# Third product of the first steps removed, small GpSimd copies moved behind the gate, and the transform of even k split once more

## The chip, the cores and the metric

The kernel runs on one NeuronCore of one Trainium2 chip. The time is device microseconds of one launch. Below, TensorE is PE (its weight loads PEld), VectorE is DVE, ScalarE is ACT, GpSimd is POOL and SyncE is SP in the profile's rows. A step's instructions wait for each other across engines by semaphores; each engine runs its own queue in program order.

## What is computed

```python
def _attn_ref(x):                      # x: 8 x 3136 x 256, float32
    X = np.fft.fft(x, axis=1)
    X = np.fft.fft(X, axis=2)
    return X.real.astype(np.float32)

def _moe_ref(x, w_in, conv_w, w_out):  # 256 -> 1024 -> 256, 3 taps
    h = np.maximum(x @ w_in, 0.0)
    hp = np.concatenate([zeros, h, zeros], axis=1)
    for k in range(3):
        conv_out += conv_w[k][None, None, :] * hp[:, k:k + S, :]
    gate = 1.0 / (1.0 + np.exp(-conv_out))
    return (h * gate @ w_out).astype(np.float32)
```

`reference` feeds the first function's output to the second. All arithmetic of the kernel is float32.

## The kernel before

**The transform.** The input is real and only the real part of the two-dimensional transform is used, so per batch two arrays are enough, for k from 0 to 1568: a cosine sum P and a sine sum Q over the sequence. The row k of h needs P and Q added, the row 3136 - k needs them subtracted. The sum over the sequence is shortened by folding: VectorE adds and subtracts the quarters of the sequence and the mirrored features (`fold_ops`, 14 pieces a batch, lines 154 to 193) until 98 (or 99) rows of the array `w` in 4 groups q are left for even k and for odd k. In the piece `feats`, GpSimd copies the one feature that has no mirror (L187, 98x4 or 99x4 elements) and clears another (L189).

A batch's transform is eight units (`units`), each of a few matrix products of a table with `w` into one PSUM bank, then a copy by ScalarE where two halves have to be combined, then two VectorE additions that write P (`pt`) or Q (`qt`). For odd k the sum over n is split into even n and odd n: `odd_even` does the n that are even, on a quarter of the k, and mirrors them (two contiguous additions, L309 and L311); `odd` does the odd n (L321 and L323, which write every second column). For even k, `even(sn, c)` takes the two classes of even k one after the other, c = 0 and c = 1, each with four products of 197 or 196 columns, one copy (L286) and two additions that write every fourth column (L290 and L293).

**The steps.** Each batch has 4 chunks of columns k and, for each chunk, 8 blocks of 128 hidden features: 32 steps a batch, 256 in all. A step s has these parts, spread over four cycles of the loop:

- `seed` (L653, ACT) writes the contribution of feature 128 to the bank `pa`.
- `products` (PE): `pb` = G1 times Q (L667), then `pa` += G0 times P.
- `copies` (ACT): `nb` gets `pb` for the front rows k and minus `pb` for the mirrored back rows, two copies (L685).
- `combine` (DVE): two custom instructions (L696), each the sum of `pa` and `nb` clipped at zero, write the front and the back of the tile `h`; `row_of` allocates `h` and clears its edges in a batch's first chunk (L663, POOL).
- `first_tap` (L702, ACT), then `tap` twice (L707, DVE, two SBUF inputs): the convolution, in the tile `g`.
- `sigmoid` (L720, ACT), in two parts.
- `gate`: g times h, the first half by VectorE (L728), the other by GpSimd (L727), with a rest by GpSimd in a batch's last chunk (L730).
- `mm2` (PE): six or more products of 256 columns with `w_out`, added up over the 8 blocks in the banks `po`, which ScalarE copies out (L747) and SP stores.

In batch 0 the steps 3 to 19 are done in another way (`triple`): PE adds `pb`'s product a third time, into `pa`, so that `pa` holds the front rows complete; ACT writes the front of `h` with a Relu (L682) and copies only minus twice `pb` for the back (L680); VectorE's L696 runs once, for the back.

**The order.** The engines' order is written out by hand. Cycle t of the loop issues `sigmoid` of step t - 2, "first" work, `products` and `copies` of step t + 1, "act" work, `combine` of step t, `seed` of t + 2, `first_tap` of t, `tap` 1 of t - 1, "dve" work, `tap` 2 of t - 1, `gate` of t - 2, "load" work, `mm2` of t - 3 and "pe" work. The named places take side work from the table `side`: the folds of batch b are spread over the cycles before `ends[b]` at "dve" (with GpSimd's L187 and L189 inside them), the units of batch b over the cycles after it (matmuls at "pe", copies at "act", additions at "dve"), and the loads of the next batch, four indirect gathers on GpSimd's queue among them (L132), at "load". Batch 1's folds lie in cycles 9 to 19 and its units in cycles 20 to 29. Cycles 0 to 9 also widen weights (L524 to L542). Batch 0's folds and units come ahead of the loop.

Of the kernel before, what the change touches and what calls it, by code (L numbers as in the profile page):

```python
# [9 lines left out]
F32 = mybir.dt.float32  # L10
# [16 lines left out]

TRIPLE = 3, 20  # L30
RC = 56
NQ = 8
CUTS = (0, 384, 768, 1152)
# [4 lines left out]
def kernel(  # L38
# [103 lines left out]
    def fold_ops(b):  # L142

        def half(h):
            k = slice(0, NP if h == 0 else KR)
            qs = slice(2 * h, 2 * h + 2)

            def t():
                return xh[b, h]

            def pair(m):
                def f():
                    a, r = t()[k, m:m + 2], t()[k, 7 - m:5 - m:-1, ::-1, :]
                    vt(a[:, :, :, 1:D], a[:, :, :, 1:D], r[:, :, :, D - 1:0:-1], op=ALU.add)  # L157
                    if m == 2:
                        a, r = t()[k, 0:4], t()[k, 7:3:-1, ::-1, :]
                        vt(a[:, :, :, 0], a[:, :, :, 0], r[:, :, :, 0], op=ALU.add)  # L160
                return f

            def flat(i, j):
                return t()[k, i:j].rearrange("p s q d -> p (s q d)")

            def both(to, op):
                def f():
                    vt(flat(to, to + 2), flat(0, 2), flat(2, 4), op=op)  # L168
                return f

            def evens():
                vt(flat(0, 1), flat(4, 5), flat(5, 6), op=ALU.add)
                vt(flat(1, 2), flat(4, 5), flat(5, 6), op=ALU.subtract)

            def feats(odd):
                def f():
                    if h == 0 and odd:
                        wt[b] = [wp.tile([P, 4, HQ, P], F32, name="w", tag="w%d" % i) for i in range(2)]
                        if b == 0:
                            ea[b] = ep.tile([P, 2, HQ], F32, name="ea", tag="ea")  # L180
# [5 lines left out]
                    vt(w[k, 2:4, qs, 0:P - 1], lo, hi, op=ALU.subtract)  # L186
# [9 lines left out]
            return [pair(0), pair(2), both(6, ALU.subtract), feats(1), both(4, ALU.add), evens,  # L196
                    feats(0)]

        return half(0) + half(1)

# [63 lines left out]
    def product(o, w, st, q, cols, start, stop):  # L264

        def f(p):
            k = KR if q == HQ - 1 else NP
            mm(p[o], w(k, q), table(k, st, q, cols), start, stop)
        return f

    def units(b):
        def w(i):
            return lambda k, q: wt[b][i // 4][0:k, i % 4, q, :]

        a_ = {}
# [91 lines left out]
        def store():  # L367
            nc.sync.dma_start(out=ed[b:b + 1, 0:NK], in_=er[b])

        return (begin, [odd_even(1), odd(1), even(1, 0), even(1, 1), feature(), odd_even(0), odd(0),  # L370
                        even(0, 0), even(0, 1)], row, flip, store)

    class Feature:

# [280 lines left out]
    def triple(s):  # L655

        return s[0] == 0 and TRIPLE[0] <= s[1] * NF + s[2] < TRIPLE[1]

    def row_of(s):
        hs[s] = hp.tile([P, HW], F32, name="h", tag="h")  # L660
        w = chunks[s[1]].w
# [3 lines left out]
    def products(s):  # L665
        b, c, f = s
        ch, n, fs = cut(s)  # L667
        pb[s] = psb.tile([P, 512], F32, name="pb", tag="pb")
        mm(pb[s][:, 0:n], G[0:P - 1, 1, fs], PQ[b][1][0:P - 1, ch.k0:ch.k1], True, True)
        mm(pa[s][:, 0:n], G[:, 0, fs], PQ[b][0][:, ch.k0:ch.k1], False, not triple(s))  # L670
        if triple(s):
            mm(pa[s][:, 0:n], G[0:P - 1, 1, fs], PQ[b][1][0:P - 1, ch.k0:ch.k1], False, True)

    def copies(s):

        ch, n, fs = cut(s)
        p = pb.pop(s)
        nb[s] = nbp.tile([P, 2, HN], F32, name="nb", tag="nb")
        if triple(s):
            act(nb[s][:, 1, ch.cols], p[:, ch.cols], AF.Copy, scale=-2.0)  # L680
            row_of(s)
            act(hs[s][:, ch.front], pa[s][:, ch.fcols], AF.Relu)  # L682
        else:
            for i, cols in enumerate((ch.fcols, ch.cols)):
                act(nb[s][:, i, cols], p[:, cols], AF.Copy, scale=-1.0 if i else 1.0)  # L685

    def combine(s):

        ch, n, fs = cut(s)
        a, c = pa.pop(s), nb.pop(s)  # L690
        if not triple(s):
            row_of(s)
        h = hs[s]
        for i, (to, cols) in enumerate(((h[:, ch.front], ch.fcols), (h[:, ch.back][:, ::-1], ch.cols))):
            if i or not triple(s):
                nc.vector._custom_dve(TENSOR_ADD_SAT, out=to, in0=a[:, cols], in1=c[:, i, cols],  # L696
                                      s0=BIG, s1=0.0)

    def first_tap(s):
        n = chunks[s[1]].w - 2  # L700
# [63 lines left out]
    begin()  # L764

    nc.gpsimd.memset(PQ[0][1][96:P, :], 0.0)
    for f in fold_ops(0):
        f()

    odds = [us[j] for j in (0, 1, 5, 6)]  # L770
# [99 lines left out]
        at(cs[-1] - 2, "load", lambda b=b: spread(b, range(len(chunks) - 1)))  # L870
        at(per * b + 1, "load", lambda b=b: spread(b, [len(chunks) - 1]))
    for b in range(1, B):
        ops = fold_ops(b)
        c0, n = ends[b - 1], ends[b] - ends[b - 1]
        cs = [free(c0 + j * n // len(ops)) if b > 1 else c0 + j * n // len(ops) for j in range(len(ops))]
        assert cs[-1] < ends[b] and (b > 1 or cs[7] > NF + 3)
# [16 lines left out]
    for t in range(n + LAG):  # L893
# [94 lines left out]
```

## Time and profile before

| | us |
|---|---|
| median of 5 runs (lowest, highest) | 1198.54 (1197.32, 1199.39) |
| the profiled execution | 1199.47 |
| its span, first to last instruction | 1197.7 |

| group | count | mean ns |
|---|---|---|
| PE L93, `po` from `wout`, 256 columns | 3072 | 379 |
| PE L93, `pb` and `pa`, 387 columns and others | 512 each | 496, 494 |
| DVE L707, the taps | 512 | 1130 |
| DVE L696, the custom sum | 495 | 558 |
| DVE L728 / POOL L727, the gate's halves | 256 / 256 | 572 / 1012 |
| ACT L685, copies of `pb` | 478 | 499 |
| ACT L682, Relu of the front, 386 and 385 columns | 17 | 493, 492 |
| POOL L187, copies of one feature | 32 | 1088 |
| POOL L189, clears | 28 | 98 |
| ACT L286, copies for even k | 32 | 322 to 331 |

A float32 product is two instructions on TensorE, and a group's mean time counts each from its start to its modelled end, so that neighbours overlap; the distance from start to start is shorter than the mean. The same holds for VectorE and ScalarE: the last 0.1 us or so of an instruction lies under the next one, and the chain of waits shows the distance. The granted TensorE clock was 1.00 in all but the last of the 30 us stretches, where work ends.

### The profile page before, as it was taken

How to read it: one execution, taken by the hardware profiler on the slowest of the kernel's cores; microseconds unless marked ns; L12 is line 12 of the kernel's file. 1: busy time of each engine (PE TensorE's matmuls, PEld its weight loads, DVE VectorE, ACT ScalarE, POOL GpSimd, SP SyncE). 2: the span in 40 equal slices, each digit the busy share in tenths (PEclk: the TensorE clock that was granted, in tenths of full speed). 3: DMA queues.
4: the chain of work that ended last, by engine and by line, in shares of the span. 5: the costliest groups of instructions: out<-in, count | busy, mean ns of one | idle time of the engine just before them, and what ended most of it. 6: DMA issues, size and time to landing. Idle time of an engine off the chain costs nothing.

```text
span 1197.7 us, 15377 instructions
## 1 busy us (share of the span) xinstructions
PE 1170.3 (98%) x4836; PEld 901.8 (75%) x4836; DVE 1128.6 (94%) x1625; ACT 884.0 (74%) x1840; POOL 476.8 (40%) x540
## 2 busy tenths in 40 slices
PE   4999999999999999999999999999999999999998
PEld 2776777777777777777777777777777777777776
DVE  7899999999999999999999999999998988899996
ACT  2677667777777777777777777777776777788884
POOL 5225556464263433624245243632234222342224
PEclk9999999999999999999999999999999999999999
DMA  9812323112031211202021010310000100110000
GB/s 220 197 35 81 82 29 107 57 54 81 1 99 41 69 39 43 79 14 81 27 88 52 27 54 27 99 36 27 27 31 24 32 27 27 47 34 27 27 27 31
DMA packets 70067, 66.07 MB, mean 55 GB/s; under 512 B 28107, under 2 KB 57683, under 8 KB 69987
## 3 DMA queue, kind: packets, MB, share of 16 engines
q1 hardware_dynamic: 64349, 51.98, 15.3%
q0 software_dynamic: 5120, 12.85, 3.5%
q8 instruction: 38, 0.62, 0.2%
q10 hardware_dynamic: 518, 0.28, 0.1%
q14 instruction: 42, 0.34, 0.1%
HBM read 39.33 MB, written 25.74 MB: 54 GB/s over the span
## 4 chain that ended last, share of the span: by engine, by line
PE 84%; DVE 11%; issue 2%; ACT 1%; POOL 1%; DMA 0%; ACTq 0%; DVEq 0%; SPq 0%; POOLq 0%
PE po L93 51%; PE pb L93 13%; PE pa L93 12%; PE pd L93 8%; DVE g L707 5%; DVE h L696 1%; DVE g L728 1%; POOL xh L132 1%; DVE xh L157 0%; ACT nb L685 0%; DVE xh L168 0%; DVE w L186 0%; DVE raw L539 0%; DVE wout L532 0%; ACT os L747 0%
## 5 line engine op out<-in xcount | busy, mean ns | idle before, releaser
L93 PE MATMUL po<-wout,g 128*128 128x256 f32 x3072 | 705.9, 379 | 5.0 <-DVE g L728 5.0
L93 PEld LDWEIGHTS po<-wout,g 128*128 128x128 f32 x3072 | 580.9, 190 | 149.3 <-issue 17.9
L707 DVE SCALAR_TENSOR_TENSOR g<-h,cw,g 128x770 f32<-128x770 f32 (+1 forms) x512 | 578.7, 1130 | 6.2 <-ACT g L702 2.4
L727 POOL TENSOR_TENSOR g<-g,h 128x385 f32<-128x385 f32 (+1 forms) x256 | 258.8, 1012 | 633.6 <-ACT g L720 439.2
L685 ACT ACTIVATE nb<-pb 128x386 f32<-128x386 f32 (+2 forms) x478 | 212.8, 499 | 162.9 <-PE pb L93 162.4
L720 ACT ACTIVATE g<-g 128x385 f32<-128x385 f32 (+2 forms) x512 | 244.6, 530 | 99.8 <-DVE g L707 96.1
L696 DVE CUSTOM_DVE_ANT_0 h<-pa,nb 128x386 f32<-128x386 f32 (+2 forms) x495 | 256.6, 558 | 3.1 <-POOL h L663 3.1
L702 ACT ACTIVATE g<-h,cw 128x770 f32<-128x770 f32 (+1 forms) x256 | 244.1, 954 | 0.0
L93 PE MATMUL pb<-qt,G 127*128 127x387 f32 (+2 forms) x512 | 212.7, 496 | 1.6 <-ACT G L622 1.6
L93 PE MATMUL pa<-pt,G 128*128 128x387 f32 (+2 forms) x512 | 211.8, 494 | 0.0
L653 ACT ACTIVATE pa<-eb,ge 128x387 f32<-128x387 f32 (+2 forms) x256 | 154.6, 604 | 0.8 <-ACT ft L458 0.6
L93 PEld LDWEIGHTS pa<-pt,G 128*128 128x128 f32 x512 | 96.8, 189 | 73.6 <-issue 18.4
L728 DVE TENSOR_TENSOR g<-g,h 128x385 f32<-128x385 f32 (+1 forms) x256 | 146.3, 572 | 3.0 <-ACT g L720 3.0
L93 PE MATMUL pd<-tab,w 98*128 98x196 f32 (+3 forms) x448 | 126.7, 374 | 0.0
L132 POOL DMA_INDIRECT xh<-in_x_dram,idx x64 | 106.3, 1662 | 13.3 <-issue 9.8
L93 PEld LDWEIGHTS pb<-qt,G 127*128 127x128 f32 x512 | 93.9, 190 | 19.6 <-ACT G L622 2.4
L93 PEld LDWEIGHTS pd<-tab,w 98*128 98x128 f32 (+1 forms) x448 | 84.7, 191 | 12.3
L730 POOL TENSOR_TENSOR left<-g,h 128x64 f32<-128x64 f32 x64 | 65.5, 1024 | 0.0
L747 ACT COPY os<-po 128x256 f32<-128x256 f32 x196 | 57.7, 392 | 9.3 <-PE po L93 4.7
L187 POOL COPY w<-xh 98x4 f32<-98x4 f32 (+1 forms) x32 | 34.8, 1088 | 39.1 <-DVE xh L168 28.4
L157 DVE TENSOR_TENSOR xh<-xh 98x1020 f32<-98x1020 f32 (+1 forms) x32 | 39.5, 1240 | 2.5 <-DMA xh<-in_x_dram,idx 2.5
L168 DVE TENSOR_TENSOR xh<-xh 98x1024 f32<-98x1024 f32 (+1 forms) x32 | 39.0, 1218 | 0.1
(118 smaller groups left out, 367.9 us busy)
## 6 DMA issues: line engine op xcount, KB each, us to landing
out_dram<-os SPq DMA_DIRECT2D x192, 128.0 KB
xh<-in_x_dram SPq DMA_DIRECT2D x16, 784.0 KB
eb<-ed SPq DMA_DIRECT2D x16, 193.5 KB
tab<-dft_seq_dram SPq DMA_DIRECT2D x4, 589.5 KB
raw<-in_moe_w_in_dram SPq DMA_DIRECT2D x4, 512.0 KB
raw<-in_moe_w_out_dram SPq DMA_DIRECT2D x1, 2048.0 KB
eb<-ed SPq DMA_DIRECT2D x8, 209.0 KB
eb<-ed SPq DMA_DIRECT2D x7, 193.0 KB
```

What stands on the lines that cost most here:

```text
L93: nc.tensor.matmul(o, l, r, start=start, stop=stop, skip_group_check=True)
L132: nc.gpsimd.indirect_dma_start(out=xh[b, h][0:NP, 7 - m].rearrange("p q d -> p (q d)"), out_offset=None, in_=bass.AP(tensor=x.tensor, offs ...
L653: act(pa[s][:, 0:n], eb[b, c], AF.Copy, scale=ge[:, f:f + 1])
L685: act(nb[s][:, i, cols], p[:, cols], AF.Copy, scale=-1.0 if i else 1.0)
L696: nc.vector._custom_dve(TENSOR_ADD_SAT, out=to, in0=a[:, cols], in1=c[:, i, cols], s0=BIG, s1=0.0)
L702: act(gs[s], hs[s][:, 0:n], AF.Copy, scale=cw[:, 0, s[2]:s[2] + 1])
L707: stt(out=g, in0=h[:, k:k + n], scalar=cw[:, k, f:f + 1], in1=g, op0=ALU.mult, op1=ALU.add)
L720: act(gs[s][:, c], gs[s][:, c], AF.Sigmoid)
L727: gt(g[:, p], g[:, p], h[:, p], op=ALU.mult)
L728: vt(g[:, v], g[:, v], h[:, v], op=ALU.mult)
L730: gt(left[:, f, b % 2 * LEFT:(b % 2 + 1) * LEFT], g[:, r], h[:, r], op=ALU.mult)
L747: nc.scalar.copy(out=osb[:, j % 2], in_=pt[:, j % 2])
```

## The change

- `triple` is gone. Steps 3 to 19 are done as all others: two products, two copies by ScalarE, two L696 on VectorE, `row_of` in `combine`.
- `feats` no longer holds GpSimd's copy and clear for batches 1 to 7. `single(odd)` does them; the loop runs it in the same cycle at a new place, "pool", which stands behind `gate` and ahead of "load". Batch 0 keeps them in `feats`.
- `even(sn, 0)` and `even(sn, 1)` become `even_even(sn)` and `even(sn)`. `even_even` takes the even n (groups q = 3 and 1) for both classes of even k on half of the columns: four products of 99 or 98 columns that write every second column of the bank, one copy by ScalarE, and two contiguous additions that make the sum and its mirror. `even` takes the odd n (q = 2 and 0): two times two products of 197 or 196 columns, again into every second column, no copy, and two additions of 393 and 392 columns that write every second column of P or Q. The number of units, of products and of additions stays; their place in the schedule too.

```diff
-TRIPLE = 3, 20
...
+            def single(odd):
+
+                def f():
+                    w, s = wt[b][odd], 6 * odd
+                    nc.gpsimd.tensor_copy(w[k, 0:2, qs, 0], t()[k, s:s + 2, :, 0])
+                    if b:
+                        nc.gpsimd.memset(w[k, 2:4, qs, P - 1:P], 0.0)
+                return f
...
-                    nc.gpsimd.tensor_copy(w[k, 0:2, qs, 0], v[:, :, :, 0])
                     if b:
-                        nc.gpsimd.memset(wt[b][odd][k, 2:4, qs, P - 1:P], 0.0)
-                    elif odd:
+                        return
+                    single(odd)()
+                    if odd:
...
+            ops = [pair(0), pair(2), both(6, ALU.subtract), feats(1), both(4, ALU.add), evens, feats(0)]
+            return ops, {3: single(1), 6: single(0)}
...
-        def even(sn, c):
-            n = HO // 2 + 1 - c
-            nh = HO // 2
-            cols = slice(c, HE, 2)
-            mms = [product((slice(0, P), slice(j * n, (j + 1) * n)), w(2 * sn + c), sn, q, cols, q == qs[0], q == qs[1])
-                   for j, qs in enumerate(((3, 1), (2, 0))) for q in qs]
+        def even_even(sn):
+
+            n = HO // 2 + 1
+            mms = [product((slice(0, P), slice(j * n + c, (j + 1) * n, 2)), w(2 * sn + c), sn, q, slice(c, n, 2),
+                           True, True) for j, q in ((0, 3), (1, 1)) for c in range(2)]
 
             def copy(p):
-                a_[sn, c] = asp.tile([P, HO + 2], F32, name="as", tag="as")
-                nc.scalar.copy(out=a_[sn, c][:, 0:n], in_=p[:, 0:n])
+                a_["v", sn], a_["e4"] = [asp.tile([P, HO + 2], F32, name="as", tag="as") for _ in range(2)]
+                nc.scalar.copy(out=a_["e4"][:, 0:n], in_=p[:, 0:n])
 
             def fin(p):
-                a, bb, t = a_[sn, c], p[:, n:2 * n], PQ[b][sn]
-                vt(t[:, 2 * c:Q4 + 1:4], a[:, 0:n], bb, op=ALU.add)
-                hi = t[:, M - 2 * c:Q4:-4]
-                x0, x1 = (bb[:, 0:nh], a[:, 0:nh]) if sn else (a[:, 0:nh], bb[:, 0:nh])
-                vt(hi, x0, x1, op=ALU.subtract)
+                a, e4, e2 = a_["v", sn], a_["e4"], p[:, n:2 * n]
+                vt(a[:, 0:n], e4[:, 0:n], e2, op=ALU.add)
+                x0, x1 = (e2[:, 0:n - 1], e4[:, 0:n - 1])[::1 if sn else -1]
+                vt(a[:, HO:n - 1:-1], x0, x1, op=ALU.subtract)
             return Unit(b, mms, copy, fin)
 
+        def even(sn):
+
+            mms = [product((slice(0, P), slice(c, HE, 2)), w(2 * sn + c), sn, q, slice(c, HE, 2), q == 2, q == 0)
+                   for c in range(2) for q in (2, 0)]
+
+            def fin(p):
+                a, bb, t = a_["v", sn][:, 0:HE], p[:, 0:HE], PQ[b][sn]
+                vt(t[:, 0:Q4 + 1:2], a, bb, op=ALU.add)
+                x0, x1 = (bb, a) if sn else (a, bb)
+                vt(t[:, M:Q4:-2], x0[:, 0:HO], x1[:, 0:HO], op=ALU.subtract)
+            return Unit(b, mms, lambda p: None, fin)
...
-        mm(pa[s][:, 0:n], G[:, 0, fs], PQ[b][0][:, ch.k0:ch.k1], False, not triple(s))
-        if triple(s):
-            mm(pa[s][:, 0:n], G[0:P - 1, 1, fs], PQ[b][1][0:P - 1, ch.k0:ch.k1], False, True)
+        mm(pa[s][:, 0:n], G[:, 0, fs], PQ[b][0][:, ch.k0:ch.k1], False, True)
...
-        if triple(s):
-            act(nb[s][:, 1, ch.cols], p[:, ch.cols], AF.Copy, scale=-2.0)
-            row_of(s)
-            act(hs[s][:, ch.front], pa[s][:, ch.fcols], AF.Relu)
-        else:
-            for i, cols in enumerate((ch.fcols, ch.cols)):
-                act(nb[s][:, i, cols], p[:, cols], AF.Copy, scale=-1.0 if i else 1.0)
+        for i, cols in enumerate((ch.fcols, ch.cols)):
+            act(nb[s][:, i, cols], p[:, cols], AF.Copy, scale=-1.0 if i else 1.0)
...
-            if i or not triple(s):
-                nc.vector._custom_dve(TENSOR_ADD_SAT, out=to, in0=a[:, cols], in1=c[:, i, cols],
-                                      s0=BIG, s1=0.0)
+            nc.vector._custom_dve(TENSOR_ADD_SAT, out=to, in0=a[:, cols], in1=c[:, i, cols], s0=BIG, s1=0.0)
...
         for j, fn in enumerate(ops):
             at(cs[j], "dve", fn)
+        for j, fn in singles.items():
+            at(cs[j], "pool", fn)
...
             gate(steps[t - 2])
+        run("pool")
         run("load")
```

More of the change, by code (lines that the diff above doesn't have):

```diff
@@ L194, in feats @@
                 return f
-            return [pair(0), pair(2), both(6, ALU.subtract), feats(1), both(4, ALU.add), evens,
-                    feats(0)]
-        return half(0) + half(1)
+            ops = [pair(0), pair(2), both(6, ALU.subtract), feats(1), both(4, ALU.add), evens, feats(0)]
+            return ops, {3: single(1), 6: single(0)}
+        (o0, s0), (o1, s1) = half(0), half(1)
+        return o0 + o1, {**s0, **{len(o0) + j: f for j, f in s1.items()}}
     tabs = [const.tile([P, n, HQ, HE], F32, name="tab%d" % n) for n in (2, 4)]
@@ L368, in store @@
             nc.sync.dma_start(out=ed[b:b + 1, 0:NK], in_=er[b])
-        return (begin, [odd_even(1), odd(1), even(1, 0), even(1, 1), feature(), odd_even(0), odd(0),
-                        even(0, 0), even(0, 1)], row, flip, store)
+        return (begin, [odd_even(1), odd(1), even_even(1), even(1), feature(), odd_even(0), odd(0),
+                        even_even(0), even(0)], row, flip, store)
     class Feature:
@@ L653, in seed @@
         act(pa[s][:, 0:n], eb[b, c], AF.Copy, scale=ge[:, f:f + 1])
-    def triple(s):
-        return s[0] == 0 and TRIPLE[0] <= s[1] * NF + s[2] < TRIPLE[1]
     def row_of(s):
@@ L690, in combine @@
         a, c = pa.pop(s), nb.pop(s)
-        if not triple(s):
-            row_of(s)
+        row_of(s)
         h = hs[s]
         for i, (to, cols) in enumerate(((h[:, ch.front], ch.fcols), (h[:, ch.back][:, ::-1], ch.cols))):
-            if i or not triple(s):
-                nc.vector._custom_dve(TENSOR_ADD_SAT, out=to, in0=a[:, cols], in1=c[:, i, cols],
-                                      s0=BIG, s1=0.0)
+            nc.vector._custom_dve(TENSOR_ADD_SAT, out=to, in0=a[:, cols], in1=c[:, i, cols], s0=BIG, s1=0.0)
     def first_tap(s):
@@ L766 @@
     nc.gpsimd.memset(PQ[0][1][96:P, :], 0.0)
-    for f in fold_ops(0):
+    for f in fold_ops(0)[0]:
         f()
@@ L872 @@
     for b in range(1, B):
-        ops = fold_ops(b)
+        ops, singles = fold_ops(b)
         c0, n = ends[b - 1], ends[b] - ends[b - 1]
```

## The prediction

> **What bounds the kernel now.** I read the engine totals first, then the engines stage by stage, then the chain of waits, then single steps in the timeline. The page's totals only say that two engines are nearly full:
>
> ```profile
> PE 1170.3 (98%) x4836; PEld 901.8 (75%) x4836; DVE 1128.6 (94%) x1625; ACT 884.0 (74%) x1840; POOL 476.8 (40%) x540
> ```
>
> The same figures by stage, with stretches cut where the chain changes engine (start:end, length, then busy time of each engine):
>
> ```profile
> core 0: us, PE busy (x) PEld busy (x) DVE busy (x) ACT busy (x) POOL busy (x), PEclk, DMA share, GB/s
> 62.50:141.30 78.80, 75.82 (x303) 54.88 (x301) 78.42 (x103) 56.25 (x131) 35.92 (x43) 1.00 0.18 55
> 141.30:185.00 43.70, 43.70 (x184) 34.02 (x185) 42.67 (x67) 29.11 (x62) 20.93 (x18) 1.00 0.39 68
> 185.00:228.00 43.00, 41.25 (x171) 29.69 (x169) 42.03 (x60) 30.25 (x63) 27.28 (x29) 1.00 0.29 83
> 228.00:1050.00 822.00, 821.69 (x3406) 640.85 (x3407) 779.31 (x1137) 627.80 (x1295) 318.13 (x350) 1.00 0.15 47
> ```
>
> Stage A (62.5 to 141.3, the 17 steps with the third product) is VectorE's: 0.38 us idle of 78.8. Stage B (to 185) is TensorE's, with 1.03 us idle on VectorE. Stage C (to 228) is VectorE's again. Stage D (to 1050) is TensorE's: 0.31 us idle in 822, VectorE 95% busy. After 1050 no transform runs and no edited operation either. In stage A the chain of waits (start, length, what) runs along VectorE:
>
> ```profile
> 86.72 1.39 DVE g L707
> ...
> 93.88 0.93 DVE g L707
> 94.81 0.47 DVE g L728
> 95.28 0.47 DVE h L696
> 95.75 1.39 DVE g L707
> ...
> 128.64 1.47 DVE w L186
> ...
> 131.98 2.16 DVE g L707
> ```
>
> The same instruction L707 takes 0.93 or 1.39 us of the chain. The timeline (start, length, instruction, idle before it) shows why, in a step with the third product at 95 us and in a plain one at 420 us:
>
> ```profile
> 95.21 0.55 DVE L696 CUSTOM_DVE_ANT_0 h<-pa,nb 128x386 f32<-128x386 f32 x1
> 95.46 0.86 POOL L727 TENSOR_TENSOR g<-g,h 128x385 f32<-128x385 f32 x1 [3.02 <-ACT g L720]
> 95.67 1.47 DVE L707 SCALAR_TENSOR_TENSOR g<-h,cw,g 128x770 f32<-128x770 f32 x1
> ```
>
> ```profile
> 420.02 1.02 DVE L696 CUSTOM_DVE_ANT_0 h<-pa,nb 128x386 f32<-128x386 f32 x2
> 420.33 0.86 POOL L727 TENSOR_TENSOR g<-g,h 128x385 f32<-128x385 f32 x1 [1.89 <-issue]
> 420.95 1.06 DVE L707 SCALAR_TENSOR_TENSOR g<-h,cw,g 128x770 f32<-128x770 f32 x1
> ```
>
> GpSimd's half of the gate begins some 0.7 us after the second tap ended. If VectorE starts a tap while it runs, the tap lasts 0.46 us longer (1.47 against 1.01); if two L696 stand in between, 0.05 us longer.
>
> **The change part by part.** *Third product, TensorE.* It issues 17 products fewer, two instructions each, which stand 0.65 us apart as a pair: 11 us less. What remains there per step is 2.59 + 1.30 = 3.89 us, 66 us for 17 steps, far below the 78.8. Worth nothing by itself, because VectorE's chain hides it.
>
> *Third product, VectorE.* Each of the 17 steps gets a second L696, 0.47 us on the chain: 17 x 0.47 = +8.0 us in stage A. Against that stands the blocked time that it fills. In the chain seven taps that follow a single L696 take 1.39 or 1.44 us (at 86.72, 90.09, 95.75, 111.57, 116.07, 120.51, 137.15) in place of 0.93; the second L696 covers 0.46 of each: -3.2. Three more, at 62.99, 72.22 and 81.38, are 0.29, 0.16 and 0.15 too long: -0.6. At 104.14 two gates of GpSimd run in a row and L707 takes 3.10; one L696 fits in there too: -0.5. The bounds are 0 covered (+8.0) and all blocked time gone: 32 taps with a mean of 1274 ns against 1.01 make 8.4 us, with L186's 0.87 (1.47 against 0.60) 9.3, so -1.3. I take the sum of the places, as each can be seen.
>
> [...]
>
> *ScalarE.* The Relu of L682 (mean 493 ns) gives way to a second copy of L685 (499): 0. The edge zeros of h are written in combine again; VectorE waited for them 3.1 us in the 64 steps that write them, so 0.05 for each of five steps, at most 0.8 each (the longest such wait): +0.2, bounds 0 and 4.
>
> *GpSimd's copies behind the gate.* 28 of the 32 copies of 1.09 us, and their memsets, move; batch 0 keeps its own. Today one stands ahead of the gate on GpSimd's queue and waits for VectorE's L168 or L173, 38 us in total; the gate and the indirect gathers queue behind it. In stage D no engine that counts waits for that (TensorE idles 0.3 us), so 0. In stage A it made the gate of 126 us come at 128.71: L186 took 1.47 for 0.60, the gather behind it 2.66, the next gate came late as well and L707 took 2.16 for 0.93. That is 2.1 us; I take -1.9. In stage C three taps are 0.6 to 0.9 too long, partly behind a copy (193.86, 204.65, 214.67): I take -0.5, bounds +0.5 and -2. What comes later now is the copy itself. Readers are the transform's products, a cycle or more later, and SP's load into the same buffer, one cycle later; gathers keep their place behind both.
>
> *Even k.* Per batch 16 products of 196 columns become 8 of 196 and 8 of 98 (pairs). Starts in the timeline:
>
> ```profile
> 402.71 0.52 PE L93 MATMUL pd<-tab,w 98*128 98x196 f32 x2
> 403.07 0.81 PE L93 MATMUL pb<-qt,G 127*128 127x387 f32 x2
> ...
> 47.02 0.95 PE L93 MATMUL po<-dm,win 128*128 128x1 f32 x8
> 47.83 0.89 PE L93 MATMUL pb<-qt,G 127*128 127x386 f32 x2
> 48.56 0.49 PE L93 MATMUL pa<-pt,G 128*128 128x386 f32 x1
> ```
>
> A pair of 196 columns takes 0.36 us (0.35 over many). 98 columns have no row. Halved by columns it would be 0.174. Eight instructions of one column, which are nearly all weight load, take 0.81 until the next product begins, and hold that one up by 0.08 (its pair takes 0.73 for the usual 0.65): 0.89 / 8 = 0.111 each, so a pair of 98 columns with such weights would take 0.22. I take this, as the row is nearest in weights and a column adds little under the load: 0.35 - 0.22 = 0.125 saved, 8 times a batch, 1.0 us. Batches 2 to 7 in stage D: -6.0; VectorE has 5% left there, so nearly all arrives: -5.7. Bounds: -8.4 (pairs at 0.174) and -3 (VectorE eats half). Batch 1 in stage B: 1.0 on TensorE, but VectorE has 1.03 idle there and must fit: -0.5, bounds -1.0 and +0.1. Batch 0 lies in the opening, where the chain runs along VectorE's widening of weights from 36.5 us on: 0, bounds -1.0 and +0.3.
>
> VectorE per batch: eight results at a start-to-start of 0.36 (2.9 us) become four of 0.27 (as L309) and four of 0.47 (as L321): 3.0 us, +0.1, counted in B. ScalarE loses two copies of 0.33 a batch; L290's waits for them (26 us in all) are VectorE's idle time in TensorE's stage and worth nothing.
>
> **Sum:** A 8.0 - 3.2 - 0.6 - 0.5 - 1.9 + 0.2 = +2.0; B -0.5; C -0.5; D -5.7; total -4.7 us. The span is 1197.7 in an execution of 1199.47, so 1.8 lies around it and stays; that execution was 0.9 above the median of 1198.54. From the median: 1193.8 us, with 1190 to 1197 if the mechanism holds.
>
> **Rivals.** *The block moves to the second tap* (slower). Place: stage A, GpSimd's gate starts inside the first tap and blocks the next. For it: the second tap at 78.60 (1.51), and after 1050, where L696 stands double and L707 still takes 1.42 at 1107.88. Against: there ScalarE is busy when a tap ends, while from 60 to 240 it waited 41 us for VectorE's taps, so its sigmoid comes at once. Price: nothing of the 4.3 and 1.9 in A is gained, nor C's 0.5: +8.2 - 0.5 - 5.7 = +2.0, 1200.5 us. It decides the sign once less than 2.0 of the 6.2 us in A are gained. *VectorE becomes the bound of stage D*: for it 95% busy, against it 42.7 us left over. Half of the saving stays out: 2.0 - 0.5 - 0.5 - 3.0 = -2.0, 1196.5. *The halved products save nothing and the strided bank writes cost*: the new units write every second column of a bank, which no row shows. If that halves the rate, pairs of 196 take 0.66: 8 x 0.31 = 2.5 us a batch, +15 in D and +2.5 in B; with A and C +19, 1217.5; against it, operands are already read at stride two at full rate. *More is unblocked*: A -1.3, B -1.0, C -1.5, D -6.2: -10.0, 1188.5.
>
> **How the numbers follow.** My sum 0.58, the block moves 0.15, VectorE bounds 0.10, strided writes 0.04, more unblocked 0.13. The time is that of the sum, 1193.8. The range 1189 to 1199.5 leaves out about half of the fastest case (0.07), most of the moved block (0.09) and the strided writes (0.04). A measurement here can tell about 0.2%, 2.4 us, from no change. Faster than 1196.1: 0.54 of my sum, 0.13, and 0.03 of VectorE's case: 0.70. Slower than 1200.9: 0.05 and 0.04: 0.09. Within: 0.21.
>
> **What would show it.** Right: taps after a double L696 in stage A at 1.0 to 1.1, no gap of several us between gates there, stage A at about 81 us; pairs of 98 columns 0.22 before the next product; TensorE still without idle time after 230. Wrong: taps of 1.4 as second ones (the block moved), VectorE without gaps in stage D, or pairs of even k above 0.35.

## The result, and the profile after

| | before | after |
|---|---|---|
| median, us (lowest to highest) | 1198.29 (1197.05 to 1200.94, 49 runs) | 1196.16 (1193.79 to 1196.93, 29 runs) |
| ratio of the times, 95% interval | | 0.9978 (0.9972 to 0.9983) |
| profiled execution, its span | 1199.47, 1197.7 | 1194.54, 1192.6 |

The changed kernel is faster by 0.22%, 2.0 to 3.4 us by the interval: in the range, on the side that was forecast, 2.4 us above the predicted 1193.8.

The engine totals of the changed kernel, first line of its page, and then its busy time by stage (start:end, length, then busy time and count for PE, PEld, DVE, ACT and POOL, granted clock, DMA). The cuts are put at the same instructions as those of before, so the lengths compare:

```profile
PE 1152.4 (97%) x4802; PEld 886.4 (74%) x4802; DVE 1134.9 (95%) x1642; ACT 878.9 (74%) x1824; POOL 476.1 (40%) x540
```

```profile
60.80:142.90 82.10, 68.57 (x271) 48.75 (x272) 80.53 (x120) 56.45 (x133) 36.17 (x41) 1.00 0.17 53
142.90:185.90 43.00, 42.70 (x184) 32.85 (x185) 42.81 (x68) 28.78 (x61) 18.69 (x20) 1.00 0.39 67
185.90:229.90 44.00, 41.25 (x170) 29.68 (x168) 42.34 (x61) 30.14 (x62) 28.28 (x29) 1.00 0.29 84
229.90:1044.90 815.00, 814.99 (x3406) 634.94 (x3407) 783.38 (x1139) 624.58 (x1283) 319.56 (x350) 1.00 0.15 47
```

Stage A is 82.1 us for 78.8, B 43.0 for 43.7, C 44.0 for 43.0, D 815.0 for 822.0. D is still TensorE's, without idle time. In A VectorE's idle time has grown from 0.4 to 1.6 us although it is the bound there: a new wait.

Stage lengths can be had more exactly from one instruction: the start of a step's first product in the changed kernel less its start in the kernel before. That difference grows by a stage's gain or loss. The table does it for the change and for its three parts, each made alone (the runs are told below); differences are taken between profiled executions, at the steps 4, 20, 28, 36 and 220.

| us | opening | A | B | C | D |
|---|---|---|---|---|---|
| predicted | 0 | +2.0 | -0.5 | -0.5 | -5.7 |
| after | -1.7 | +3.3 | -0.6 | +1.0 | -7.0 |
| third product out, alone (e2) | -1.7 | +3.6 | +0.5 | 0.0 | 0.0 |
| copies behind the gate, alone (e3) | -0.7 | -0.3 | 0.0 | +0.9 | 0.0 |
| new units, alone (e1) | -2.1 | 0.0 | -1.1 | +0.1 | -6.9 |
| sum of the three, without the opening | | +3.3 | -0.6 | +1.0 | -6.9 |

From A on, the parts add up to the whole within 0.1 us. One entry needs care. Step 3 no longer has its third product, so in the changed kernel and in e2 TensorE starts step 4 by 0.56 us earlier for that alone (at step 3 the differences are -1.2 and -1.1), and in stage B it gives this back (+0.5 in e2). So the third product's removal costs 3.6 + 0.5 - 0.56 = 3.5 us in all, and counted from step 3 the whole change gains 3.9 us up to the end, where 4.7 were predicted.

The opening does not add up, because it differs between executions of one kernel: a second profile of the changed kernel, e7, stands at +0.6 at step 3 where the first has -1.2, while its stages agree with the first's within 0.1 us; e1 and its second profile, e8, stand at -2.1 and -0.1, and their stages agree as well. One difference is TensorE's rate: its instructions of 512 columns start 0.85 us apart up to 22.5 us in the profiled execution of before, up to 19.5 in that of after and up to 22.2 in e7, and 0.43 us apart behind these times. (The windows of before and after show a granted clock of 1.00 on both sides; "full clock" for what begins there is the author's reading.) Another is a stretch at half clock, told below. So the two profiled executions differ by 4.9 us and the medians by 2.1, and what a typical execution does in the opening is better taken as the difference of the medians less that of the stages from step 3 on: for the changed kernel -2.1 + 3.9 = +1.8 us.

### The profile page after: what moved, and what is told of

The parts are those of the page before. It is cut to its first block, busy times and chain, and to the rows that moved or that the text cites. A ratio compares the mean times of both kernels' runs of the same rounds, so it can differ in the third digit from the quotient of the medians.

```text
span 1192.6 us, 15307 instructions
## 1 busy us (share of the span) xinstructions
PE 1152.4 (97%) x4802; PEld 886.4 (74%) x4802; DVE 1134.9 (95%) x1642; ACT 878.9 (74%) x1824; POOL 476.1 (40%) x540
## 4 chain that ended last, share of the span: by engine, by line
PE 84%; DVE 5%; issue 3%; ACT 2%; POOL 2%; DMA 0%; ACTq 0%; POOLq 0%; DVEq 0%; SPq 0%
PE po L92 51%; PE pb L92 13%; PE pa L92 13%; PE pd L92 7%; DVE g L712 2%; DVE h L702 1%; POOL xh L131 1%; DVE g L733 1%; ACT nb L693 0%; ACT os L752 0%; ACT g L725 0%; POOL left L735 0%; POOL g L732 0%; DVE w L194 0%; ACT pa L672 0%
## 5 line engine op out<-in xcount | busy, mean ns | idle before, releaser
L732 POOL TENSOR_TENSOR g<-g,h 128x385 f32<-128x385 f32 (+1 forms) x256 | 275.2, 1075 | 671.5 <-ACT g L725 468.7
L693 ACT ACTIVATE nb<-pb 128x386 f32<-128x386 f32 (+3 forms) x512 | 227.5, 498 | 182.9 <-PE pb L92 182.4
L702 DVE CUSTOM_DVE_ANT_0 h<-pa,nb 128x386 f32<-128x386 f32 (+3 forms) x512 | 264.6, 558 | 6.5 <-POOL h L678 6.5
L92 PE MATMUL pd<-tab,w 98*128 98x196 f32 (+3 forms) x448 | 118.4, 356 | 0.0
L92 PEld LDWEIGHTS pb<-qt,G 127*128 127x128 f32 x512 | 91.0, 190 | 19.9 <-ACT G L641 2.7
L178 POOL COPY w<-xh 98x4 f32<-98x4 f32 (+1 forms) x32 | 20.6, 643 | 6.1 <-DVE xh L167 3.6
```

The lines of the kernel that those rows point to most:

```text
L92: nc.tensor.matmul(o, l, r, start=start, stop=stop, skip_group_check=True)
L732: gt(g[:, p], g[:, p], h[:, p], op=ALU.mult)
```

## The experiments

Each run's times stand against runs of the kernel before on the same chip, whose medians were 1198.2 to 1198.7.

### The three parts, each alone

**e1**: the kernel before with `even_even` and `even` in place of `even(sn, 0)` and `even(sn, 1)`, nothing else.

```diff
-        return (begin, [odd_even(1), odd(1), even(1, 0), even(1, 1), feature(), odd_even(0), odd(0),
-                        even(0, 0), even(0, 1)], row, flip, store)
+        return (begin, [odd_even(1), odd(1), even_even(1), even(1), feature(), odd_even(0), odd(0),
+                        even_even(0), even(0)], row, flip, store)
```

> The kernel before with the new units for even k alone. Theory 1 (the sum, resized by the profile after): TensorE's stage from 230 to 1050 gives 7.0 us (six batches at 1.17), the opening up to 1.5; 1190 to 1192 us, granted clock 1.000 in all executions since the third product keeps TensorE busy. Rival (the opening's gain is given back before the long stage, as VectorE sets the first 17 steps): 1191.3, with the start of the long stage unchanged. Rival (lower clock comes from the shorter weight-bound products): 1193 to 1194 with the clock at 0.996 to 0.998.

Measured: 1192.01 (1189.48 to 1192.42), ratio 0.9949 (0.9936 to 0.9963). The units alone gain more than the whole change does. The granted clock was 1.000 in one execution of five, not in all as the theory has it. In stage D a profile of TensorE shows the halved products. The timeline of the changed kernel, TensorE alone, in two cycles of batch 2's units (start, length, instruction):

```profile
386.51 0.37 PE L92 MATMUL pd<-tab,w 99*128 99x98 f32 x2
386.71 0.84 PE L92 MATMUL pb<-qt,G 127*128 127x387 f32 x2
387.38 0.81 PE L92 MATMUL pa<-pt,G 128*128 128x387 f32 x2
388.04 2.75 PE L92 MATMUL po<-wout,g 128*128 128x256 f32 x12
390.62 0.37 PE L92 MATMUL pd<-tab,w 98*128 98x99 f32 x2
```

The pair of 98 columns holds its place for 0.20 us, and the next pair takes 0.67 for its usual 0.65: 0.22 in all, as worked out. The cycle is 4.11 us (386.51 to 390.62), where one with 196 columns takes 4.25 (402.71 to 406.96 in the kernel before). Eight of them a batch and six batches make 8 x 6 x 0.14 = 6.7 us; 6.9 to 7.0 were measured.

**e2**: the kernel before without `triple`.

```diff
-        if triple(s):
-            mm(pa[s][:, 0:n], G[0:P - 1, 1, fs], PQ[b][1][0:P - 1, ch.k0:ch.k1], False, True)
...
-            if i or not triple(s):
-                nc.vector._custom_dve(TENSOR_ADD_SAT, out=to, in0=a[:, cols], in1=c[:, i, cols],
-                                      s0=BIG, s1=0.0)
+            nc.vector._custom_dve(TENSOR_ADD_SAT, out=to, in0=a[:, cols], in1=c[:, i, cols], s0=BIG, s1=0.0)
```

> The kernel before without the third product, nothing else. Theory 1: 17 more sums on VectorE cost 8.0 us and fill about 4.3 us of blocked time; late gates behind GpSimd's copies stay: +3.5 to +4.5 us of span, taps that follow a sum at 1.0 to 1.1 us. Rival (the block moves to the second tap): +8 us, 1206. Clock theory (TensorE, now idle between products in these steps, is granted half its clock for some us in most executions): the median lies 2 to 3 us above what the span of a profile with a clock of 1.000 says, granted clock 0.996 to 0.998; without it the clock is 1.000.

Measured: 1201.92 (1201.14 to 1203.48), ratio 1.0032 (1.0019 to 1.0044). Taking the third product out makes the kernel slower by itself: +3.6 us in stage A, 3.5 in all.

**e3**: the kernel before with GpSimd's copy and clear behind the gate.

```diff
-                    nc.gpsimd.tensor_copy(w[k, 0:2, qs, 0], v[:, :, :, 0])
...
+        run("pool")
         run("load")
```

> The kernel before with GpSimd's copies behind the gate, nothing else. Theory 1: the late gates of the steps around 128 and 132 us go, 1.5 to 2 us in the first 17 steps, nothing from 230 on: 1196.3 to 1197. Rival (TensorE's queue sets these steps at 4.55 us each, so that VectorE's blocked time is waited for anyway): no change, 1198.3.

Measured: 1200.04 (1197.48 to 1201.07), ratio 1.001 (1.0001 to 1.0019): no gain, and rather a loss. It gains 0.3 us in A and loses 0.9 in C, which makes 0.6 of the 1.6 us by which its median is longer; the rest is not in the stages of its profile and stays open. The loss in C has one place. The timeline of e3 in stage C, GpSimd alone, and then two lines of VectorE (the last field is idle time and what ended it):

```profile
204.40 1.10 POOL L740 TENSOR_TENSOR left<-g,h 128x64 f32<-128x64 f32 x1
205.46 0.64 POOL L179 COPY w<-xh 99x4 f32<-99x4 f32 x1
206.04 0.09 POOL L181 MEMSET w<- 99x4 f32 x1
206.32 2.68 POOL L132 DMA_INDIRECT xh<-in_x_dram,idx  x1 [0.19 <-issue]
209.01 0.12 POOL L673 MEMSET h<- 128x2 f32 x1
```

```profile
207.56 0.55 DVE L738 TENSOR_TENSOR g<-g,h 128x384 f32<-128x384 f32 x1
209.16 1.03 DVE L706 CUSTOM_DVE_ANT_0 h<-pa,nb 128x385 f32<-128x385 f32 x2 [1.05 <-POOL h L673]
```

The same part of GpSimd's queue in the kernel before, and VectorE's sum behind it:

```profile
205.63 1.08 POOL L730 TENSOR_TENSOR left<-g,h 128x64 f32<-128x64 f32 x1
206.91 1.25 POOL L132 DMA_INDIRECT xh<-in_x_dram,idx  x1 [0.19 <-issue]
208.16 0.12 POOL L663 MEMSET h<- 128x2 f32 x1
209.24 1.02 DVE L696 CUSTOM_DVE_ANT_0 h<-pa,nb 128x385 f32<-128x385 f32 x2
```

The copy now stands between the gate's rest and the gather. The gather takes 2.68 us for 1.25 (why, was not tried), and behind it on the same queue waits the clearing of the edges of `h`, which comes at 209.01. VectorE's sum needs those edges and idles for 1.05 us, in a stage that VectorE bounds. In the kernel before it did not wait there. The changed kernel repeats it 2.05 us later: clearing at 211.06, 1.05 us idle.

**e4**: the changed kernel with `triple` kept, so e1 and e3 together.

> The changed kernel with the third product kept in steps 3 to 19. Theory 1: 7.0 us from the long stage, 1.5 to 2 from the copies, 0 to 1 from the opening: 1188.5 to 1190, clock 1.000; it beats both kernels. Rival (the third product's removal is what pays, since VectorE's blocked time is filled by its sum): 1194 or more, above the changed kernel's profiled 1194.5.

Measured: 1191.8 (1191.07 to 1192.41), ratio 0.9948 (0.9934 to 0.9961). By stage: A -0.3, B -1.1, C +1.0, D -6.9. With the third product in place the rest of the change is 4.4 us below the changed kernel's median, and no faster than the units alone. The expected 1188.5 to 1190 counted on 1.5 to 2 us from the copies, which do not come.

### Does the second sum hide under GpSimd's gate?

The prediction holds that a second L696 in a step costs little where it fills time in which GpSimd's gate would block the first tap. To tell this from a sum that costs 0.47 us wherever it is, **e6** takes the changed kernel and puts the second sum of steps 3 to 19 behind the first tap of the step before, so that a tap again follows a single sum.

```diff
+            combine(steps[t], (0,) if late else (0, 1))
+        if late:
+            if 0 <= t - 1 < n:
+                tap(steps[t - 1], 1)
+            combine(steps[t], (1,))
...
-        if 0 <= t - 1 < n:
+        if 0 <= t - 1 < n and not late:
```

> The changed kernel, in which steps 3 to 19 issue their second sum on VectorE behind the first tap in place of ahead of it; same work. Block theory (the second sum costs little because it runs while GpSimd's half of the gate would block the tap): the first taps take 1.4 to 1.5 us again, blocked time in the first 17 steps rises from 4.0 to 8 to 10 us, span 1196 to 1198. Rival (the sum costs little for another reason, such as TensorE's shorter steps): 1193 to 1194, taps at 1.0 to 1.1.

Measured: 1201.58 (1198.78 to 1202.48), ratio 1.0021 (1.0012 to 1.0031): 5.4 us above the changed kernel, with the same instructions. That is more than the 1196 to 1198 expected. By the profiles stage A is 4.7 us longer than in the changed kernel (+8.0 against +3.3) and stage B 0.7. First the timeline of the changed kernel, VectorE and GpSimd, and then that of e6:

```profile
90.48 1.02 DVE L702 CUSTOM_DVE_ANT_0 h<-pa,nb 128x386 f32<-128x386 f32 x2
...
90.79 0.86 POOL L732 TENSOR_TENSOR g<-g,h 128x385 f32<-128x385 f32 x1 [2.57 <-issue]
...
91.42 1.05 DVE L712 SCALAR_TENSOR_TENSOR g<-h,cw,g 128x770 f32<-128x770 f32 x1
```

```profile
85.40 0.55 DVE L707 CUSTOM_DVE_ANT_0 h<-pa,nb 128x385 f32<-128x385 f32 x1
85.72 0.87 POOL L737 TENSOR_TENSOR g<-g,h 128x385 f32<-128x385 f32 x1 [3.22 <-ACT g L730]
85.87 1.53 DVE L717 SCALAR_TENSOR_TENSOR g<-h,cw,g 128x770 f32<-128x770 f32 x1
...
87.33 0.55 DVE L707 CUSTOM_DVE_ANT_0 h<-pa,nb 128x385 f32<-128x385 f32 x1
```

Behind two sums the tap takes 1.05 us, behind one 1.53, while the gate starts 0.3 us after the first sum in both. All of stage A can be added up in this way. For each line and shape on VectorE the fastest tenth of the distances from one start to the next, where nothing idles between, is what the instruction takes unblocked; what the others take above it is blocked time. In stage A it is 10.1 us before, 4.0 after, 4.4 in e2, 9.7 in e3 and in e4, 9.2 in e6. VectorE's idle time there is 1.5 us in e6 and 1.6 in the changed kernel, so e6's 4.7 us are blocked time and no new wait. The 17 sums cost 17 x 0.47 = 8.0, blocked time falls by 6.1, VectorE's new idle time is 1.2: 8.0 - 6.1 + 1.2 = 3.1 of the measured 3.3.

The 1.2 us of idle time are one wait. The waits of VectorE in the changed kernel's stage A (us in total, times, longest), and then the timeline at that place:

```profile
DVE h L702 <- POOL h L678: 1.2, 1, 1.2
```

```profile
76.56 0.19 POOL L421 TENSOR_SCALAR ft<-ft 128x2 f32<-128x2 int32 x1 [4.93 <-DVE ft L420]
76.70 0.90 POOL L429 MEMSET ft<- 1x393 f32 x4
...
77.54 0.09 POOL L678 MEMSET h<- 128x2 f32 x1
77.60 0.86 POOL L732 TENSOR_TENSOR g<-g,h 128x385 f32<-128x385 f32 x1
77.66 1.03 DVE L702 CUSTOM_DVE_ANT_0 h<-pa,nb 128x385 f32<-128x385 f32 x2 [1.19 <-POOL h L678]
```

With the third product, `h` was allocated and its edges cleared in `copies`, the better part of a cycle earlier (for this step at 71.53 in the kernel before). Now the clearing is issued by `combine`, right ahead of the sum that needs it, and it stands behind GpSimd's work for the special feature (L421, L429).

### Why do the copies behind the gate gain nothing in stage A?

The prediction took the late gate of 126 us for the cause of 2.1 us of blocking. In the changed kernel that gate is no longer late, it starts as soon as its sigmoid releases it. The timeline, VectorE and GpSimd:

```profile
126.70 1.01 DVE L702 CUSTOM_DVE_ANT_0 h<-pa,nb 128x386 f32<-128x386 f32 x2
...
126.96 3.55 POOL L732 TENSOR_TENSOR g<-g,h 128x385 f32<-128x385 f32 x1 [2.73 <-ACT g L725]
...
127.64 1.00 DVE L712 SCALAR_TENSOR_TENSOR g<-h,cw,g 128x770 f32<-128x770 f32 x1
...
128.57 1.21 DVE L167 TENSOR_TENSOR xh<-xh 99x1024 f32<-99x1024 f32 x1
...
129.82 1.24 DVE L193 TENSOR_TENSOR w<-xh 99x508 f32<-99x508 f32 x1
...
131.34 2.62 POOL L131 DMA_INDIRECT xh<-in_x_dram,idx  x1 [0.19 <-issue]
...
133.91 1.78 DVE L712 SCALAR_TENSOR_TENSOR g<-h,cw,g 128x770 f32<-128x770 f32 x1
133.99 0.87 POOL L732 TENSOR_TENSOR g<-g,h 128x385 f32<-128x385 f32 x1
```

An instruction that takes 0.87 us takes 3.55: a tap and two folds of VectorE, each later in its start, pass in about their usual time, the last with 0.57 more. GpSimd is late from here on as it was in the kernel before: the gather takes 2.62, the next gate comes at 133.99 inside a tap, and the tap takes 1.78. In e3 the same gate starts at 124.91, takes 3.08, and the tap at 130.93 takes 2.24. So the late start was a companion of the blocking rather than its cause: with the start moved ahead, the same tap and folds of VectorE still pass first. By the rows an earlier start does not settle which of the two is held up: the gate of 90.79 starts 0.63 us ahead of its tap and takes 0.86, the gate of e6 at 85.72 starts 0.15 ahead and takes 0.87 while the tap takes 1.53, and the gate of 126.96, 0.68 ahead of its tap, takes 3.55. Why the last one lost and the others did not was not tried; a row's start on GpSimd is a rough time in these profiles, so it need not be the moment at which the gate began to read.

### The clock in the opening

In most executions of the changed kernel the mean granted clock was 0.995 to 0.997 (23 of 31), in most of the kernel before 0.999. One theory was TensorE's idle time in stage A, which went from 3.0 to 13.5 us. **e5** gives TensorE its work back: in steps 3 to 19 `pb`'s product is issued twice, the second one over the first.

```diff
-        mm(pb[s][:, 0:n], G[0:P - 1, 1, fs], PQ[b][1][0:P - 1, ch.k0:ch.k1], True, True)
+        for _ in range(2 if b == 0 and 3 <= c * NF + f < 20 else 1):
+            mm(pb[s][:, 0:n], G[0:P - 1, 1, fs], PQ[b][1][0:P - 1, ch.k0:ch.k1], True, True)
```

> The changed kernel, in which TensorE issues pb's product twice in steps 3 to 19 (the second overwrites the first with the same numbers), so that it is as busy there as before while VectorE's work is that of the changed kernel. Clock theory (the changed kernel's executions lose 1 to 3 us where TensorE, idle for 13 us in these steps, is granted half its clock for windows of 3.4 us, as the trace without the third product shows one at 114 us): granted clock 0.999 in all executions, median 1193.5 to 1194.5, 2 us below the changed kernel's. Rival (the lower clock comes from somewhere else): clocks of 0.996 to 0.998 stay and the median stays at 1196 or rises by TensorE's extra work.

Measured: 1196.7 (1194.18 to 1197.47), ratio 0.9985 (0.9976 to 0.9994), granted clock 0.995 to 0.997 in nine of eleven executions. Filling stage A mends nothing. Second profiles of the changed kernel and of the units alone, **e7** and **e8**, without an edit, were taken to see where the clock falls.

> The changed kernel again, for a trace of an execution with a granted clock of 0.996 to 0.998. Clock theory: stretches of half clock between 62 and 141 us, some 3.4 us each, one for 0.9975 and two for 0.996. Rival: they lie in the opening before 60 us or in the long stage, beside the products of 98 columns.

> The kernel before with the new units alone, again, for a trace of an execution with a clock of 0.996 to 0.998 (four of the five had one, and were 2.3 to 2.9 us longer than the one at 1.000). Theory: a half-clock stretch in the opening, where the weight-bound products of 98 columns run in a row. Rival: in the first 17 steps, or in the long stage.

Measured: 1196.37 and 1191.42. Both have a stretch of 3.4 us at half clock in the opening (from 42.7 us in e7, 41.8 in e8), e7 another from 114.4. Here is TensorE's timeline in e8 at that place, with the windows around it (length, busy times, the granted clock third from the end):

```profile
34.82 4.86 PE L93 MATMUL po<-tab,w 99*128 99x99 f32 x32
39.91 0.91 PE L93 MATMUL pd<-er,one 1*128 1x386 f32 x2 [0.23 <-POOL er L362]
41.04 1.12 PE L93 MATMUL po<-dm,win 128*128 128x1 f32 x8 [0.23 <-issue]
42.23 3.45 PE L93 MATMUL po<-win,dm 128*128 128x256 f32 x8
```

```profile
41.00:42.00 1.00, 0.96 (x8) 0.99 (x8) 0.96 (x3) 0.33 (x1) 0.95 (x1) 0.91 1.07 410
42.00:43.00 1.00, 0.94 (x3) 0.79 (x4) 0.90 (x4) 0.16 (x1) 0.70 (x2) 0.50 0.76 283
```

The eight instructions of 256 columns take 3.45 us; in the first profile of the changed kernel, at full clock, they take 1.96. TensorE has no gap above 0.3 us in the 7 us before. What it does there is small: the new units of batch 0, in one row of 32 instructions that shows the first's shape (sixteen have 98 or 99 columns, sixteen 196 or 197), then a product with one row of weights and eight instructions of one column.

**e9** and **e10** put one product of 512 columns, read by nobody, ahead of the eight instructions of one column, in the changed kernel and in the units alone.

```diff
+    keep_on([idle] * 1)
```

> The changed kernel with one product of 512 columns, whose result nobody reads, issued in the opening between the transform's last row and the first block of w_in, where TensorE waits 0.8 us. Theory (the changed kernel's slower executions lose 1.8 to 2.8 us because TensorE, less busy between 38 and 42 us with the products of 98 columns, is granted half its clock in the next window): no half-clock stretch before 60 us in most executions, median 1194.0 to 1194.8, granted clock 0.998 or 0.999 (a window around 114 us may stay and costs nothing). Rival (the half clock is set by the shape of the products and not by the gap): clock 0.996 as before, median 1196.3 to 1197.2.

> The kernel before with the new units alone and the same filling product. Theory: 0.999 to 1.000 in most executions, median 1189.3 to 1190.3, 2 us under the new units alone and the fastest version here. Rival: 1192 as without the filling product, or 0.9 us more where VectorE was waiting for the block it delays.

Measured: 1196.16 (1193.99 to 1199.22), ratio 0.9982 (0.9973 to 0.999), and 1191.55 (1190.93 to 1192.33), ratio 0.9941 (0.9928 to 0.9954): medians as without the product. In e9 six of twelve executions had 0.998 where eight of 31 of the changed kernel have that or more; in e10 three of five had the clock at 1.0 and two at 0.998, where the units alone have one of five at 1.0. But these three took 1190.9 to 1191.6, not 1189.5, and e10's profile still has the stretch, from 42.5 us. That left open whether the new units are the cause at all. **e11** and **e12** use the new units in batches 1 to 7 only, and the old ones in batch 0, which lies in the opening: e11 is e1 with this edit, e12 the changed kernel.

```diff
+        ev = [(even_even(sn), even(sn)) if b else (even_old(sn, 0), even_old(sn, 1)) for sn in range(2)]
+        return (begin, [odd_even(1), odd(1), *ev[1], feature(), odd_even(0), odd(0), *ev[0]], row, flip, store)
```

> The kernel before with the new units of even k in batches 1 to 7 only; batch 0, which lies in the opening, keeps the old ones. Theory: the products of 98 columns in the opening are what brings TensorE's half-clock window of 3.4 us at about 42 us, which most executions of the units alone had (granted clock .996 to .998 in four of five, 1191.8 to 1192.4, and 1189.5 in the one with 1.0). Then all five executions show .998 or more and the median is 1189.5 to 1190.5. Rival: the window comes whatever the units are (the opening has other small products ahead of it): clock and median as with the units alone, 1191.4 to 1192.4. Second rival: batch 0's units gain something in the opening themselves (its profiles stood 1.5 us ahead there): 1193 or more.

> The changed kernel with the new units of even k in batches 1 to 7 only. Theory (the window at 42 us comes from the new units in the opening, and costs the changed kernel 1.8 us up to step 4, most of which stays): granted clock .998 or more in most executions, median 1194.2 to 1195.0. Rival (the window has another cause, or what is late in the opening is made up in the stage that VectorE bounds): 1195.8 to 1196.6, clock .995 to .997 as before this edit.

Measured: e11 1191.1 (1190.57 to 1192.18), ratio 0.9936 (0.9923 to 0.995), clock 1.0 in four of five executions; e12 1195.02 (1193.07 to 1196.91), ratio 0.9969 (0.996 to 0.9979), clock 0.998 or more in eight of ten. So the theory's clocks came out. The profiles say the same: none of the five with the old units in batch 0 (before, e2, e3, e11, e12) has the stretch in the opening, four of the nine with the new ones do (e6, e7, e8, e10). In these four the full clock came at 21.3 us or later, in the four without it and without the filler (after, e1, e4, e5) by 20.0; with the old units it came at 21.2 to 22.5 and no stretch followed. So in these profiles the stretch goes with both, the new units and a late full clock (e9, with the filler and 21.8 us, has none). The units were tried by e11 and e12; the late clock was not, and why the two should matter is not shown. Nor was a slower execution of the kernel before (1200 us and more, clock 0.998) profiled.

What it costs can be read from the start of batch 0's even units (the row of 32 instructions) to step 0's first product. That takes 10.0 to 10.2 us with the old units, 9.8 to 10.3 with the new ones and no stretch, and 11.3 to 12.0 with it. So the stretch costs 1.0 to 2.2 us up to there (most in e6, where it lasts 6.8 us), and the new units save next to nothing there, though their row is 4.85 us for 5.89.

The theory's times were too good: 0.9 and 1.1 us are gained, where 1.5 to 2.5 and 1.2 to 2.0 were expected. For e11 they went by e1's one execution at full clock, 1189.48, and its profile is 1.0 us ahead of e11's already where these units begin (33.71 against 34.70 us; full clock from 19.2 against 21.2). For e12 they went by the two profiles of the changed kernel, whose full clock came at 19.5 and 22.2. The gains in the medians are about as large as the spread of the runs, and the intervals overlap with those of e1 and of the change. Taken as above, medians less stages from step 3 on, the opening is 0.0, 0.1 and 0.2 us longer than before in e2, e11 and e12 (e3, 1.0, is the exception) and 0.7 to 2.1 longer in the seven kernels with the new units in batch 0 (e4 the least, e5 the most).

The profile of e12 has no half clock in the opening and still one stretch of 3.4 us from 114.1 on, in stage A. It follows a real gap; TensorE's rows there:

```profile
109.41 0.81 PE L92 MATMUL pa<-pt,G 128*128 128x387 f32 x2
113.03 4.52 PE L92 MATMUL po<-wout,g 128*128 128x256 f32 x12 [2.81 <-DVE g L752]
```

The first profile of the changed kernel has the same gap there and keeps the full clock, so the twelve instructions take 2.86 us for 4.52:

```profile
112.56 2.86 PE L92 MATMUL po<-wout,g 128*128 128x256 f32 x12 [2.81 <-DVE g L733]
```

So the gap does not decide it alone. Such a stretch at 114 us is also in the profiles of e2, e7 and e9, and one at 93 us in that of e6, which all lack the third product; after and e5 lack it too and have none, and none is in those that keep it (before, e1, e3, e4, e8, e10, e11). Where VectorE bounds the stage it costs nothing later: e12's stage A is +3.3, as that of the first profile of the changed kernel, which had none.

## Why the prediction came out, point by point

**Even k, stage D: right in its mechanism, a little too small.** The pair of 98 columns was sized 0.22 from the products of one column, and takes 0.22. Predicted -5.7, measured -7.0. Stage B, predicted -0.5 because VectorE would eat half, gains the whole: -1.1 in e1. The saving a product is 0.14 rather than 0.125, and the discount for VectorE's 5% was not needed: VectorE went to 96% (783.4 of 815), TensorE stayed without idle time. Some 0.3 us of the 7.0 are not accounted for by the pairs. The rival of VectorE as the bound of D falls, and so does that of strided bank writes: an instruction of 196 columns on 98 partitions, which now writes every second column, has a mean of 333 ns in D, 334 before.

**Third product: right, by two errors that cancel.** Its own sum was 8.0 - 4.3 + 0.2 = +3.9 in stage A; e2 measured +3.6 there and 3.5 in all. More blocked time was covered than the places added up to, 5.7 for 4.3 us. The edges' clearing, taken at +0.2, cost 1.2 in a single wait: the bound (0 to 4) held it, but the reason was missed, which is that the clearing moves on GpSimd's queue behind the special feature's work. The rival in which the block moves to the second tap falls: blocked time goes and comes with the place of the second sum (4.0 us in the changed kernel, 9.2 in e6), and A did not lose the 8.2 us of that rival. The opposite rival, more unblocked, with A at -1.3, falls as well.

**The copies behind the gate: the step that failed.** "It made the gate of 126 us come at 128.71 ... That is 2.1 us; I take -1.9" gave 0.3 us (e3, stage A). The gate came on time and then took 3.55 us, while VectorE's tap and folds passed; the gather and the next gate were as late as before. The -0.5 of stage C became +0.9: the price of the moved copy for what is queued behind it (gather, then clearing, then VectorE's sum) was named as a change of place only, "gathers keep their place behind both". They do, and are later. These two are 1.6 + 1.4 = 3.0 us too little. The even units (-0.6 in B, -1.3 in D) and the third product (-0.4) go against it, so that from step 3 on -3.9 came for -4.7; that it is so near is partly luck. The rest of the miss, 1.8 us, lies in the opening.

**The opening, taken at 0 with bounds of -1.0 and +0.3: the other step that failed.** The reason for the 0 holds, the chain runs along VectorE and the shorter products save next to nothing there. That they could cost something was not seen: a stretch at half clock, in four of the nine profiles with the new units in batch 0. By the medians of e1 and e11 the new units of batch 0 cost 0.9 us, by those of the changed kernel and e12 1.1, both with runs that overlap; by the medians less the stages it is 1.8 for the changed kernel, where 0.3 was the bound.

Parts that beat both kernels: the new units without the other two edits (e1 1192.0), e4 about as much, and best with batch 0 left as it was (e11 1191.1, 0.9936 of before, some 5 us below the changed kernel). The third product was worth keeping: it saves 3.5 us of VectorE's time and is paid for with TensorE time that is hidden.

## What to carry to other kernels

A late instruction may be a symptom of the instructions that run beside it on another engine, as GpSimd's gate of 126 us, which came on time in the changed kernel and took 3.55 us for 0.87 beside VectorE's tap and folds: before a queue is rearranged to make it early, read what the other engine does in the time that it would then fall into. When work is moved on a queue, follow all that is queued behind its new place up to the engine that bounds the stage, even for instructions of 0.1 us such as a clearing. And a change in three parts is best judged part by part: here one gains 8 us in the loop, one loses 3.5, one is worth nothing, and the whole shows 0.2%.

## What the hardware showed that was not expected

TensorE's granted clock fell to half (0.50 in the windows) for 3.4 us while TensorE was busy: in e8 from 41.8 us on, with no gap above 0.3 us in the 7 us before, after small products. The stretch of e12 from 114.1 us on, as long, follows a gap of 2.81 us, which the first profile of the changed kernel passed at full clock. What brings the clock down is not shown.

A GpSimd instruction that by its row started first took until three VectorE instructions that came after it had passed or begun (3.55 us for 0.87, from 126.96 us in the changed kernel).
